# Row-order key loads, an activation in three instructions and paired PSUM banks in a fused window-attention and feed-forward kernel

## The chip, the cores and the metric

The kernel runs on one core of one Trainium2 chip. The metric is device time in microseconds (us) from the first to the last instruction of the launch, as the median of several runs. The core's engines are named as in the profile: PE (TensorE, matrix products), PEld (its weight loads), DVE (VectorE), ACT (ScalarE), POOL (GpSimd, which here also issues the input DMAs) and SP (SyncE, which issues the output DMAs). Each engine works through its own instructions in program order and waits on semaphores for the others.

## What is computed

Eight batches of eight heads, 576 positions, 64 dimensions: attention in a symmetric window of 32 positions, then a feed-forward layer with a smooth ReLU ("SMELU") on the 4608 tokens of 512 features. Cut to what matters:

```python
def _attn_ref(q, k, v):                      # (8, 8, 576, 64) each
    scores = (1.0 / np.sqrt(D)) * np.matmul(q, k.transpose(0, 1, 3, 2))
    mask = np.abs(pos[:, None] - pos[None, :]) <= 32
    scores = np.where(mask, scores, -1000000000.0)
    attn = np.exp(scores - np.max(scores, axis=-1, keepdims=True))
    attn = attn / (np.sum(attn, axis=-1, keepdims=True) + 1e-09)
    return np.matmul(attn, v)

def _moe_ref(x, w_in, w_out):                # (4608, 512), (512, 2048), (2048, 512)
    h = x @ w_in
    g = np.where(h >= 1, h, np.where(h <= -1, 0.0, (h + 1) ** 2 / 4.0))
    return g @ w_out                         # x: heads side by side, (4608, 512)
```

## The kernel before

All matrix work is in bf16 with fp32 sums. The program is one list of slots, `a` from -1 on, and each engine executes its instructions in the order in which the slots write them (a manual schedule; no planner reorders). A slot of the steady part holds, in this order on PE: four matmuls of the first layer into one PSUM bank `hp` (L257), one group of score matmuls into `sc` (L180), four matmuls of the second layer into `op` (L277), and either a group of transposes into `tp` (L152) or the denominators and numerators of half a head pair, `dn` and `nm` (L197, L198, L206). Attention runs ahead of the feed-forward layer by 29 slots: slots -1 to 28 hold attention alone, the first layer starts in slot 29, the second layer 16 slots later, attention ends in slot 139, the first layer in slot 172, and 16 slots of the second layer alone close the program. The pattern repeats every eight slots, which handle one `m`, that is four heads in two pairs `i`; a slot with `a` odd has a `dn`/`nm` half, an even one a transpose group, and every slot but multiples of four has scores.

What feeds PE, by engine:

- POOL issues the loads of `qn`, `kn` (L89, two each for one `m`) and `vz` (L96, two for one `i`), converting to bf16, at the start of fixed slots: `q` and `k` of one `m` every eight slots, `v` of one `i` every four. Between them it multiplies the exponentials by the window's mask (L189). DMAs issued by POOL go round eight landing semaphores, so each issue waits until the eighth last has landed.
- `q` and `k` are loaded with nine consecutive positions for each partition (p j order), which makes long runs in DRAM. DVE then copies them to `qj` and `kj` so that two heads stand side by side (the relay, L140); PE transposes 9 blocks of 128x128 in two groups (5 and 4 blocks) for each of `q` and `k`; DVE evacuates the transposed `q` to `qT` (L157, one copy of 640 or 512 elements a group) and ACT the transposed `k` to the zero-padded `kz` (L164, four copies of 64 partitions a group), both scattering elements with a stride so that positions come out in order.
- ACT takes the exponentials `pt` (L188) and the reciprocals of the denominators as exp(-ln) (`lr`, `rc`, L212 and L213); DVE multiplies `nm` by `rc` into `xT` (L217), the feed-forward layer's input, one slot after `nm` was written.
- SMELU is written as max(h,-1) + (0.5 min(max(h,-1),1) - 0.5)^2: DVE clamps `hp` to `c` (L260), ACT squares it to `s` (L268), and DVE adds max(hp,-1) in the next slot to give `gT` (L271).
- ACT evacuates `op` to `osb` every fourth slot (L281) and SP sends it out (L283).

The eight PSUM banks are three for `hp` and one each for `op`, `sc`, `tp`, `nm` and `dn`. A bank is written again only when its reader has finished.

## Time and profile before

| What | us |
|---|---|
| Median of 3 runs | 472.46 (472.14 to 472.97) |
| The profiled execution | 473.16 |
| Its span, first to last instruction | 471.4 |
| PE busy | 347.5 (74%) |
| DVE busy | 311.1 (66%) |
| ACT busy | 268.9 (57%) |
| POOL busy, computing and issuing | 175.0 (37%) |

A share of the whole span is an average over stages: the loading and the first attention slots, two rounds of eight slots with the first layer but without the second, ten rounds with everything, the rounds in which attention fades out, the two layers alone, and the second layer alone. So the profile is read stage by stage. A round takes eight slots, and where nothing but PE limits it the starts of consecutive groups of matmuls follow each other without a gap; a gap has a releaser, which the trace names.

### The profile page before, as it was taken

How to read it: one execution, taken by the hardware profiler on the slowest of the kernel's cores; microseconds unless marked ns; L12 is line 12 of the kernel's file. 1: busy time of each engine (PE TensorE's matmuls, PEld its weight loads, DVE VectorE, ACT ScalarE, POOL GpSimd, SP SyncE). 2: the span in 40 equal slices, each digit the busy share in tenths (PEclk: the TensorE clock that was granted, in tenths of full speed). 3: DMA queues.
4: the chain of work that ended last, by engine and by line, in shares of the span. 5: the costliest groups of instructions: out<-in, count | busy, mean ns of one | idle time of the engine just before them, and what ended most of it. 6: DMA issues, size and time to landing. Idle time of an engine off the chain costs nothing.

```text
span 471.4 us, 6061 instructions
## 1 busy us (share of the span) xinstructions
PE 347.5 (74%) x2176; PEld 183.1 (39%) x2176; DVE 311.1 (66%) x441; ACT 268.9 (57%) x533; POOL 175.0 (37%) x236
## 2 busy tenths in 40 slices
PE   0135458567979787878787879787878999798976
PEld 0024334333535343434343435343444543343432
DVE  5633556868777777777777777777776666666610
ACT  1057557575767666666666666666667743333320
POOL 8647586262717171717171726232223200000000
PEclk9999999895999999999999989999999999999999
DMA  9999873343445353535363626220000010101011
GB/s 97 170 160 177 116 76 37 39 42 35 52 69 63 60 69 52 69 53 78 43 76 45 88 33 89 32 37 22 24 22 24 22 46 22 45 24 42 26 44 67
DMA packets 54909, 28.17 MB, mean 60 GB/s; under 512 B 39520, under 2 KB 49760, under 8 KB 54880
## 3 DMA queue, kind: packets, MB, share of 16 engines
q0 software_dynamic: 49696, 18.36, 35.1%
q1 hardware_dynamic: 5184, 9.44, 5.4%
q8 instruction: 17, 0.28, 0.2%
q14 instruction: 12, 0.10, 0.1%
HBM read 36.70 MB, written 9.44 MB: 98 GB/s over the span
## 4 chain that ended last, share of the span: by engine, by line
PE 39%; ACT 23%; DVE 19%; issue 15%; POOL 2%; ACTq 0%; DVEq 0%; POOLq 0%
PE op L277 18%; PE hp L257 13%; ACT kz L164 11%; DVE c L260 10%; ACT s L268 6%; ACT osb L281 4%; DVE qT L157 4%; DVE gT L271 3%; PE tp L152 3%; ACT pt L188 2%; PE nm L206 2%; PE sc L180 1%; POOL vz L96 1%; DVE xT L217 1%; PE dn L197 1%
## 5 line engine op out<-in xcount | busy, mean ns | idle before, releaser
L277 PE MATMUL op<-w_out,gT 128*128 128x512 bf16 x576 | 148.3, 384 | 36.2 <-ACT osb L281 36.2
L271 DVE SCALAR_TENSOR_TENSOR gT<-hp,s 128x512 bf16<-128x512 f32 x144 | 104.3, 724 | 104.4 <-ACT s L268 104.4
L268 ACT ACTIVATE s<-c 128x512 f32<-128x512 f32 x144 | 90.5, 628 | 137.7 <-DVE c L260 137.2
L257 PE MATMUL hp<-xT,w_in 128*128 128x512 bf16 x576 | 153.8, 390 | 2.0 <-DVE xT L217 1.8
L189 POOL TENSOR_TENSOR pt<-pt,maskp 128x352 bf16<-128x352 bf16 (+1 forms) x96 | 84.3, 881 | 185.5 <-ACT pt L188 185.0
L260 DVE TENSOR_SCALAR c<-hp 128x512 f32<-128x512 f32 x144 | 97.8, 679 | 3.5 <-PE hp L257 3.5
L164 ACT COPY kz<-tp 64x320 bf16<-64x320 bf16 (+1 forms) x128 | 77.4, 711 | 31.2 <-PE tp L152 30.9
L157 DVE COPY qT<-tp 128x640 bf16<-128x640 bf16 (+1 forms) x32 | 86.3, 2696 | 9.7 <-PE tp L152 9.7
L277 PEld LDWEIGHTS <-gT 128*128 128x128 bf16 x576 | 54.6, 98 | 93.8 <-issue 44.2
L257 PEld LDWEIGHTS <-w_in 128*128 128x128 bf16 x576 | 53.3, 100 | 45.8 <-issue 4.6
L96 POOL DMA_DIRECT2D vz<-in_v_dram x64 | 50.0, 789 | 11.2 <-DMA w_in<-in_moe_w_in_dram 10.4
L188 ACT ACTIVATE pt<-sc 128x352 bf16<-128x352 f32 (+1 forms) x96 | 44.7, 465 | 12.0 <-PE sc L180 11.1
L180 PE MATMUL sc<-qT,kz 128*128 128x128 bf16 (+1 forms) x288 | 34.1, 233 | 17.7 <-ACT pt L188 17.7
L180 PEld LDWEIGHTS <-kz 128*128 128x128 bf16 x288 | 25.7, 107 | 44.8 <-issue 29.5
L152 PE MATMUL tp<-ident,qj 128*128 128x128 bf16 x144 | 15.1, 240 | 33.9 <-DVE qj L140 16.4
L217 DVE TENSOR_TENSOR xT<-nm,rc 128x288 bf16<-128x288 f32 x64 | 29.1, 454 | 15.0 <-ACT rc L213 9.0
L152 PE MATMUL tp<-ident,kj 128*128 128x128 bf16 x144 | 15.4, 243 | 26.4 <-DVE kj L140 23.8
L206 PE MATMUL nm<-pt,vz 128*128 128x128 bf16 (+2 forms) x320 | 29.1, 228 | 2.1 <-DVE xT L217 2.1
L213 ACT ACTIVATE rc<-lr 128x288 f32<-128x288 f32 x64 | 28.3, 443 | 2.0
L281 ACT COPY osb<-op 128x512 f32<-128x512 f32 x36 | 20.5, 569 | 14.9 <-PE op L277 14.9
L152 PEld LDWEIGHTS <-qj 128*128 128x128 bf16 x144 | 11.9, 107 | 40.8 <-DVE qj L140 18.4
L206 PEld LDWEIGHTS <-vz 128*128 128x128 bf16 x320 | 23.3, 107 | 9.5 <-issue 5.9
(29 smaller groups left out, 160.2 us busy)
## 6 DMA issues: line engine op xcount, KB each, us to landing
out_dram<-osb SPq DMA_DIRECT2D x36, 256.0 KB, 2.0
qn<-in_q_dram POOLq DMA_DIRECT2D x32, 144.0 KB, 3.3
kn<-in_k_dram POOLq DMA_DIRECT2D x32, 144.0 KB, 5.2
vz<-in_v_dram POOLq DMA_DIRECT2D x64, 72.0 KB, 3.4
w_in<-in_moe_w_in_dram POOLq DMA_DIRECT2D x1, 2048.0 KB, 15.6
w_out<-in_moe_w_out_dram POOLq DMA_DIRECT2D x1, 2048.0 KB, 15.3
```

What stands on the lines that cost most here:

```text
L96: nc.gpsimd.dma_start(out=vz[i % 8][h:128:2, :, 64 * h:64 * h + 64], in_=v[b, 2 * hp + h].rearrange("(c p) d -> p c d", p=64))
L152: nc.tensor.transpose(ps[:, j - j0], src[:, j].rearrange("p h d -> p (h d)"), ident)
L157: nc.vector.tensor_copy(qT[m].rearrange("d g (p j) -> d j g p", j=NC)[:, j0:j1], ps[:, :n].rearrange("d j (g p) -> d j g p", g=2))
L164: nc.scalar.copy(kz[2 * (m % 2) + g][r].rearrange("d (p j t) -> d t p j", j=NC, t=2)[:, h, :, j0:j1], ps[r, :n].rearrange("d j (g p) -> d ...
L180: nc.tensor.matmul(ps[:, off:off + q1 - q0], kz[2 * (m % 2) + gg][:, 128 * c:128 * c + 128], qT[m][:, gg, q0:q1], start=True, stop=True)
L189: nc.gpsimd.tensor_mul(pt[i][:, seg], pt[i][:, seg], maskp[:, seg])
L206: nc.tensor.matmul(nm[:, q0 - lo:q1 - lo], vz[i % 8][:, c], pt[i][:, pcol(c, q0):pcol(c, q1)], start=n == 0, stop=n == len(parts) - 1, ski ...
L257: nc.tensor.matmul(hp, w_in[:, kk, 128 * f:128 * f + 128], xT[:, kk, TB * blk:TB * blk + TB], start=kk == 0, stop=kk == 3)
L260: nc.vector.tensor_scalar(c1, hp, -1.0, 1.0, op0=ALU.max, op1=ALU.min)
L268: nc.scalar.activation(s1, c1, AF.Square, scale=0.5, bias=-0.5)
L271: nc.vector.scalar_tensor_tensor(gT[blk][:, f], hp, -1.0, s1, op0=ALU.max, op1=ALU.add)
L277: nc.tensor.matmul(op, gT[blk - 1][:, ff, 128 * tt:128 * tt + 128], w_out[:, ff], start=ff == 0, stop=ff == 15)
```

## The change

- `k` is loaded in row order (64 consecutive positions over the partitions, nine chunks), one DMA for each head, so four issues instead of two for one `m`; `kn` then has the layout that the transposes read, and the relay of `k` falls away. `v` and `k` stand in two halves of 64 partitions, one for each head, instead of interleaved, and the masks and the matrix of ones are built for that.
- The relay of `q` moves from DVE to POOL.
- `qT` is evacuated by ACT (two copies a group), `kz` by DVE (four copies a group, contiguous runs of 64).
- SMELU becomes max(h,r) min(r,1) with r = relu(0.5 h + 0.5) from ACT (`rr`), then two DVE instructions in the same slot: `yy` = max(hp, rr) and `gT` = min(rr,1) yy.
- PSUM: `hp` has two banks instead of three, `op` two instead of one, and `sc` and `tp` share two (one tag) instead of having one each.

```diff
-    ps_h = ctx.enter_context(tc.tile_pool(name="ps_h", bufs=3, space=bass.MemoryType.PSUM))
-    ps_o = ctx.enter_context(tc.tile_pool(name="ps_o", bufs=1, space=bass.MemoryType.PSUM))
-    ps_s = ctx.enter_context(tc.tile_pool(name="ps_s", bufs=1, space=bass.MemoryType.PSUM))
-    ps_t = ctx.enter_context(tc.tile_pool(name="ps_t", bufs=1, space=bass.MemoryType.PSUM))
+    ps_h = ctx.enter_context(tc.tile_pool(name="ps_h", bufs=2, space=bass.MemoryType.PSUM))
+    ps_o = ctx.enter_context(tc.tile_pool(name="ps_o", bufs=2, space=bass.MemoryType.PSUM))
+    ps_s = ctx.enter_context(tc.tile_pool(name="ps_s", bufs=2, space=bass.MemoryType.PSUM))
...
+        for g in range(2):
+            for h in range(2):
+                nc.gpsimd.dma_start(out=kn[m][64 * g:64 * g + 64, :, h],
+                                    in_=k[b, 4 * qd + 2 * g + h].rearrange("(c p) d -> p c d", p=64))
...
-                out=vz[i % 8][h:128:2, :, 64 * h:64 * h + 64],
+                out=vz[i % 8][64 * h:64 * h + 64, :, 64 * h:64 * h + 64],
...
-    def relay(m, t):
-
-        src, dst = ((qn, qj), (kn, kj))[t // 2]
-        dst[m] = qkj.tile([128, NC, 2, D], BF, name="qj" if t < 2 else "kj")
-        nc.vector.tensor_copy(dst[m].rearrange("p j h d -> p h j d"),
-                              src[m].rearrange("p h (j d) -> p h j d", d=D))
+    def relay(m):
+
+        qj[m] = qjp.tile([128, NC, 2, D], BF, name="qj")
+        nc.gpsimd.tensor_copy(qj[m].rearrange("p j h d -> p h j d"),
+                              qn[m].rearrange("p h (j d) -> p h j d", d=D))
...
-        ps = ps_t.tile([128, 5, 128], BF, name="tp")
+        ps = ps_s.tile([128, 5, 128], BF, name="tp", tag="sc")
...
-                nc.vector.tensor_copy(
-                    qT[m].rearrange("d g (p j) -> d j g p", j=NC)[:, j0:j1],
-                    ps[:, :n].rearrange("d j (g p) -> d j g p", g=2))
...
+        if t < 2:
+            for g in range(2):
+                nc.scalar.copy(
+                    qT[m][:, g].rearrange("d (p j) -> d p j", j=NC)[:, :, j0:j1],
+                    ps[:, :n].rearrange("d j (g p) -> d g p j", g=2)[:, g])
+        else:
+            for h in range(2):
+                for g in range(2):
                     r = slice(64 * h, 64 * h + 64)
...
+                    nc.vector.tensor_copy(kz[2 * (m % 2) + g][r, j0:j1, h],
+                                          ps[r, :n].rearrange("d c (g p) -> d g c p", g=2)[:, g])
...
-            if t % 2 == 0:
-                att_r[8 * m + 2 * t - 1] = (m, t)
+        att_r[8 * m - 1] = m
...
-            c1 = ewp.tile([128, TB], FP, name="c1")
-            nc.vector.tensor_scalar(c1, hp, -1.0, 1.0, op0=ALU.max, op1=ALU.min)
+
+            rr = ewp.tile([128, TB], FP, name="rr")
+            yy = ewp.tile([128, TB], FP, name="yy")
+            nc.scalar.activation(rr, hp, AF.Relu, scale=0.5, bias=0.5)
+            nc.vector.tensor_max(yy, hp, rr)
+            nc.vector.scalar_tensor_tensor(gT[blk][:, f], rr, 1.0, yy, op0=ALU.min, op1=ALU.mult)
```

On POOL, at the end of the start-up loads, before:

```order
L96 DMA vz_118<-in_v_dram 64x9x64 x2
L131 DMA w_out<-in_moe_w_out_dram 128x16x512
L89 DMA qn<-in_q_dram 64x2x576 x2
L89 DMA kn<-in_k_dram 64x2x576 x2
L189 TENSOR_TENSOR pt<-pt,maskp 128x352 x2
```

And now, at the same place:

```order
L97 DMA vz_115<-in_v_dram 64x9x64 x2
L129 DMA w_out<-in_moe_w_out_dram 128x16x512
L137 COPY qj<-qn 128x2x9x64 x2
L87 DMA qn<-in_q_dram 64x2x576 x2
L91 DMA kn<-in_k_dram 64x9x64 x4
L182 TENSOR_TENSOR pt<-pt,maskp 128x352 x2
```

The relays of the first two `m`, on which PE's first transposes wait, now stand on POOL behind all start-up loads; before they stood on DVE.

On POOL, one later round of eight slots, before:

```order
L189 TENSOR_TENSOR pt<-pt,maskp 128x384
L89 DMA qn<-in_q_dram 64x2x576 x2
L89 DMA kn<-in_k_dram 64x2x576 x2
L189 TENSOR_TENSOR pt<-pt,maskp 128x352
L96 DMA vz_113<-in_v_dram 64x9x64 x2
L189 TENSOR_TENSOR pt<-pt,maskp 128x352
```

And now:

```order
L182 TENSOR_TENSOR pt<-pt,maskp 128x384
L137 COPY qj<-qn 128x2x9x64
L87 DMA qn<-in_q_dram 64x2x576 x2
L91 DMA kn<-in_k_dram 64x9x64 x4
L182 TENSOR_TENSOR pt<-pt,maskp 128x352
L97 DMA vz_110<-in_v_dram 64x9x64 x2
```

A relay and two more DMA issues stand between the mask product that ends one round and the one that opens the next.

On DVE, a stretch of the same stage around a `q` evacuation, before (`c` and `s` carry running numbers):

```order
L260 TENSOR_SCALAR c_1643<-hp 128x512
L217 TENSOR_TENSOR xT<-nm,rc 128x288
L157 COPY qT<-tp 128x5x128
L271 SCALAR_TENSOR_TENSOR gT<-hp,s_1646 128x512
L260 TENSOR_SCALAR c_1669<-hp 128x512
```

And now around a `k` evacuation:

```order
L248 TENSOR_TENSOR yy<-hp,rr 128x512
L249 SCALAR_TENSOR_TENSOR gT<-rr,yy 128x512
L208 TENSOR_TENSOR xT<-nm,rc 128x288
L160 COPY kz_106<-tp 64x5x64
L160 COPY kz_107<-tp 64x5x64
L160 COPY kz_106<-tp 64x5x64
L160 COPY kz_107<-tp 64x5x64
L248 TENSOR_TENSOR yy<-hp,rr 128x512
```

The product `gT` follows its own slot's `yy` at once, and `xT` comes behind both; the one long copy is replaced by four short ones.

## Rows read from the trace of the kernel before

**Rows 1.** Six stages: us, busy of PE, PEld, DVE, ACT, POOL; PEclk, DMA share, GB/s.

```profile
0.00:69.50 69.50, 22.64 (x170) 17.02 (x171) 37.03 (x49) 28.33 (x56) 48.40 (x73) 1.00 1.06 135
69.50:114.10 44.60, 29.88 (x195) 15.91 (x193) 32.79 (x45) 28.73 (x58) 21.32 (x28) 0.90 0.40 40
114.10:346.60 232.50, 189.94 (x1282) 101.28 (x1281) 173.80 (x241) 157.42 (x320) 97.44 (x126) 0.98 0.38 53
346.60:384.20 37.60, 33.83 (x218) 17.75 (x216) 25.18 (x42) 27.05 (x55) 7.85 (x9) 1.00 0.08 29
384.20:451.00 66.80, 56.71 (x257) 24.98 (x256) 42.12 (x67) 25.04 (x42) 0.00 (x0) 1.00 0.09 32
451.00:471.50 20.50, 14.45 (x64) 6.14 (x63) 0.22 (x1) 2.34 (x4) 0.00 (x0) 0.97 0.17 64
```

**Rows 2.** Timeline of PE in one round: start us, us, engine, line, operation.

```profile
214.20 0.33 PE L180 MATMUL sc<-qT,kz 128*128 128x128 bf16 x3
214.36 1.03 PE L277 MATMUL op<-w_out,gT 128*128 128x512 bf16 x4
215.23 0.29 PE L197 MATMUL dn<-pt,ones 128*128 128x288 bf16 x1
...
215.70 1.03 PE L257 MATMUL hp<-xT,w_in 128*128 128x512 bf16 x4
...
217.43 0.44 PE L152 MATMUL tp<-ident,qj 128*128 128x128 bf16 x5
217.70 1.03 PE L257 MATMUL hp<-xT,w_in 128*128 128x512 bf16 x4
```

**Rows 3.** Waits of the whole span: who for whom, us in total, times, longest.

```profile
PE op L277 <- ACT osb L281: 36.2, 34, 2.0
```

**Rows 4.** Groups of instructions: count, busy us, mean ns, idle before and its releaser.

```profile
L271 DVE SCALAR_TENSOR_TENSOR gT<-hp,s 128x512 bf16<-128x512 f32 x144 | 104.3, 724 | 104.4 <-ACT s L268 104.4
L268 ACT ACTIVATE s<-c 128x512 f32<-128x512 f32 x144 | 90.5, 628 | 137.7 <-DVE c L260 137.2
...
L260 DVE TENSOR_SCALAR c<-hp 128x512 f32<-128x512 f32 x144 | 97.8, 679 | 3.5 <-PE hp L257 3.5
L164 ACT COPY kz<-tp 64x320 bf16<-64x320 bf16 (+1 forms) x128 | 77.4, 711 | 31.2 <-PE tp L152 30.9
L157 DVE COPY qT<-tp 128x640 bf16<-128x640 bf16 (+1 forms) x32 | 86.3, 2696 | 9.7 <-PE tp L152 9.7
...
L188 ACT ACTIVATE pt<-sc 128x352 bf16<-128x352 f32 (+1 forms) x96 | 44.7, 465 | 12.0 <-PE sc L180 11.1
...
L217 DVE TENSOR_TENSOR xT<-nm,rc 128x288 bf16<-128x288 f32 x64 | 29.1, 454 | 15.0 <-ACT rc L213 9.0
...
L189 POOL TENSOR_TENSOR pt<-pt,maskp 128x352 bf16<-128x352 bf16 x64 | 55.1, 862 | 149.6 <-ACT pt L188 149.2
...
L189 POOL TENSOR_TENSOR pt<-pt,maskp 128x384 bf16<-128x384 bf16 x32 | 29.4, 919 | 35.8 <-ACT pt L188 35.8
...
L89 POOL DMA_DIRECT2D kn<-in_k_dram x32 | 19.5, 626 | 1.7 <-DMA w_out<-in_moe_w_out_dram 1.6
```

**Rows 5.** Start-up on PE and POOL: start us, us, operation, idle before and its releaser.

```profile
16.37 0.71 PE L152 MATMUL tp<-ident,qj 128*128 128x128 bf16 x5 [16.37 <-DVE qj L140]
```

**Rows 6.** Start-up on POOL alone, the large loads: start us, us, operation.

```profile
13.97 0.78 POOL L127 DMA_DIRECT2D w_in<-in_moe_w_in_dram  x1
...
29.83 3.78 POOL L96 DMA_DIRECT2D vz<-in_v_dram  x5 [10.39 <-DMA w_in<-in_moe_w_in_dram]
33.57 1.20 POOL L131 DMA_DIRECT2D w_out<-in_moe_w_out_dram  x1
```

**Rows 7.** The relay of `k` on DVE: duration min/median/max, first and last start.

```profile
L140 DVE COPY kj<-kn x16: 436/448/1660, 22.8 to 345.8; 128x1152 bf16<-128x1152 bf16 x16
```

**Rows 8.** Timeline around the longest of them: start us, us, engine, operation.

```profile
51.73 1.66 DVE L140 COPY kj<-kn 128x1152 bf16<-128x1152 bf16 x1
52.20 1.96 POOL L189 TENSOR_TENSOR pt<-pt,maskp 128x352 bf16<-128x352 bf16 x2
```

More of the change, by code (lines that the diff above doesn't have):

```diff
@@ L52 @@
     qkn = ctx.enter_context(tc.tile_pool(name="qkn", bufs=3))
-    qkj = ctx.enter_context(tc.tile_pool(name="qkj", bufs=2))
+    qjp = ctx.enter_context(tc.tile_pool(name="qjp", bufs=2))
     qtp = ctx.enter_context(tc.tile_pool(name="qtp", bufs=2))
@@ L73 @@
     xT = const.tile([128, 4, NT], BF, name="xT")
-    kz = [const.tile([128, 2 * S], BF, name=f"kz{i}") for i in range(4)]
+    kz = [const.tile([128, NC, 2, 64], BF, name=f"kz{i}") for i in range(4)]
     vz = [const.tile([128, NC, 128], BF, name=f"vz{i}") for i in range(8)]
@@ L83, in load_qk @@
         b, qd = divmod(m, 2)
-        for src, dst, nm in ((q, qn, "qn"), (k, kn, "kn")):
-            t = qkn.tile([128, 2, S], BF, name=nm)
-            dst[m] = t
-            for g in range(2):
-                h0 = 4 * qd + 2 * g
-                nc.gpsimd.dma_start(
-                    out=t[64 * g:64 * g + 64],
-                    in_=src[b, h0:h0 + 2].rearrange("h (p j) d -> p h (j d)", j=NC))
+        qn[m] = qkn.tile([128, 2, S], BF, name="qn")
+        kn[m] = qkn.tile([128, NC, 2, D], BF, name="kn")
+        for g in range(2):
+            h0 = 4 * qd + 2 * g
+            nc.gpsimd.dma_start(out=qn[m][64 * g:64 * g + 64],
+                                in_=q[b, h0:h0 + 2].rearrange("h (p j) d -> p h (j d)", j=NC))
+        for g in range(2):
+            for h in range(2):
+                nc.gpsimd.dma_start(out=kn[m][64 * g:64 * g + 64, :, h],
+                                    in_=k[b, 4 * qd + 2 * g + h].rearrange("(c p) d -> p c d", p=64))
     def load_v(i):
@@ L118 @@
         nc.vector.tensor_copy(maskp[:, pcol(c, q0):pcol(c, q0) + q1 - q0], mask1[:, j0:j0 + q1 - q0])
-    nc.gpsimd.memset(ones2, 1.0)
-    ev = smp.tile([128, 64, 2], FP, name="ev")
-    par = smp.tile([128, 2], FP, name="par")
-    nc.vector.tensor_copy(ev, ident.rearrange("p (a b) -> p a b", b=2))
-    nc.vector.reduce_sum(par, ev.rearrange("p a b -> p b a"), axis=mybir.AxisListType.X)
-    for h in range(2):
-        nc.vector.tensor_scalar_mul(ones2[:, 64 * h:64 * h + 64], ones2[:, 64 * h:64 * h + 64], par[:, h:h + 1])
     nc.gpsimd.dma_start(out=w_in, in_=moe_w_in.rearrange("(ko ki) f -> ki ko f", ki=128))
@@ L174, in scores @@
             pt[i] = ptp.tile([128, PW], BF, name="pt")
-        ps = ps_s.tile([128, 512], FP, name="sc")
+        ps = ps_s.tile([128, 512], FP, name="sc", tag="sc")
         off = 0
@@ L185, in scores @@
         seg = slice(first, first + off)
-        def finish():
-            nc.scalar.activation(pt[i][:, seg], ps[:, :off], AF.Exp, scale=D ** -0.5)
-            nc.gpsimd.tensor_mul(pt[i][:, seg], pt[i][:, seg], maskp[:, seg])
-        return finish
+        nc.scalar.activation(pt[i][:, seg], ps[:, :off], AF.Exp, scale=D ** -0.5)
+        nc.gpsimd.tensor_mul(pt[i][:, seg], pt[i][:, seg], maskp[:, seg])
     def pv(i, hf):
@@ L207, in pv, with mul @@
                              start=n == 0, stop=n == len(parts) - 1, skip_group_check=True)
-        def act():
-            lr = smp.tile([128, HALF], FP, name="lr")
-            rc = smp.tile([128, HALF], FP, name="rc")
-            nc.scalar.activation(lr, dn, AF.Ln)
-            nc.scalar.activation(rc, lr, AF.Exp, scale=-1.0)
-            def mul():
-                b, hp = divmod(i, H // 2)
-                nc.vector.tensor_mul(xT[:, hp, b * S + lo:b * S + hi], nm, rc)
-            return mul
-        return act
+        lr = smp.tile([128, HALF], FP, name="lr")
+        rc = smp.tile([128, HALF], FP, name="rc")
+        nc.scalar.activation(lr, dn, AF.Ln)
+        nc.scalar.activation(rc, lr, AF.Exp, scale=-1.0)
+        def mul():
+            b, hp = divmod(i, H // 2)
+            nc.vector.tensor_mul(xT[:, hp, b * S + lo:b * S + hi], nm, rc)
+        return mul
     A0 = 9
@@ L264 @@
         if a in att_s:
-            scores(*att_s[a])()
-        if hp is not None:
-            s1 = ewp.tile([128, TB], FP, name="s1")
-            nc.scalar.activation(s1, c1, AF.Square, scale=0.5, bias=-0.5)
-            def stt(hp=hp, s1=s1, blk=blk, f=f):
-                nc.vector.scalar_tensor_tensor(gT[blk][:, f], hp, -1.0, s1, op0=ALU.max, op1=ALU.add)
+            scores(*att_s[a])
         if 1 <= blk <= NBLK and mm >= 0:
@@ L284 @@
         if a in att_r:
-            relay(*att_r[a])
+            relay(att_r[a])
         if a in att_x:
```

42 lines of the change are left out of this document (17 added, 25 removed).

## The prediction

> **What bounds the kernel now.** I read the six stages first, then the chain of waits, then PE's timeline inside one round, then the costliest groups. Ten rounds of eight slots take 232.5 us, 23.25 each, in which PE is busy 19.0, DVE 17.4, ACT 15.7 and POOL 9.7 [rows 1]: no engine fills the round, so something between them does. PE's own need comes from its timeline where nothing holds it [rows 2]: `op` to `dn` is 0.87 us and an `hp` group costs the same, `sc` 0.16, a `dn`/`nm` half 0.47, a transpose group of five blocks 0.27, one of four in proportion 0.22. A round is 16 x 0.865 + 6 x 0.16 + 4 x 0.47 + 1.0 = 17.7 us. The other 5.6 us are waits of PE: for the single `op` bank until ACT has emptied it (36.2 us in all, 34 times) [rows 3], and for transposes behind one `tp` bank, which is emptied by `qT` copies of 2.7 us on DVE or by four `kz` copies of 0.71 us on ACT [rows 4], with the activation's own steps queued behind these. In the stage with the two layers alone the same bank shows undiluted: 66.8 us for 32 slots [rows 1], 2.09 each against 2 x 0.865 = 1.73.
>
> **The change, part by part, in one steady round.** *PE* does the same matmuls, 17.7 us. *DVE* loses two `qT` copies (5.4 us) and two relays (0.45 each at the median [rows 7]). It gains eight `kz` copies, which no row shows. A 288-element read of PSUM takes 0.454 us and a 512-element one 0.679 [rows 4], 1.0 ns an element, so 320 and 256 elements are 0.49 and 0.42: eight come to 3.6; half of that, 1.8, is the lower bound if packed bf16 goes at two elements a step, as the relay does at better than two; I take 3.2. `yy` is priced as `c` (0.679) and `gT` stays at 0.72, but `gT` now waits for the `yy` just ahead of it, so the two no longer overlap with their neighbours: about 1.36 a slot, 10.9 a round. With four `xT` (1.8) that is 15.9 us. *ACT* loses eight `kz` copies (5.7 us) and gains four `qT` copies; they read the same pattern at 128 instead of 64 partitions, so 0.71 each is the row for them (0.46, what an exponential of 352 or 384 elements takes, is the other end [rows 4]): 15.7 - 5.7 + 2.8 = 12.8. The relu is priced as the square, 0.63 [rows 4], and no longer waits for DVE.
>
> *POOL* gains the relay of `q` and two DMA issues. Four `kn` issues in the form of `vz`, 3.78 / 5 = 0.76 us [rows 6], replace two of 0.626 [rows 4]: +1.8. The relay on POOL is the unknown. The mask product's two sizes, 352 and 384 elements, take 0.862 and 0.919 [rows 4]: 1.78 ns an element and 0.24 fixed. At that rate 1152 elements cost 2.3 us; with one operand to read instead of two, half the slope, 1.3. I take 1.7. POOL is then 9.7 + 1.8 + 1.7 = 13.2 busy.
>
> So PE's 17.7 is the floor and DVE comes next. Two things keep a round above it. First, the relay stands in POOL's queue behind the mask product of slot 7 and ahead of the six DMA issues of the next round. Slot 7 begins; `hp` is there after 1.1 us, the relu takes 0.6, the exponential 0.5, the mask product 0.9: 3.1, with the relay 4.8. PE reaches the transposes after slot 7 (0.865 + 0.16 + 0.865 + 0.47) and two groups of the next, at 4.1, so it waits about 0.8 with handovers (nothing at a relay of 1.0 us, 1.4 at 2.3). Behind it on POOL the six issues (4.3 us) end before PE needs the next mask products. `kn` can be loaded only when PE has transposed the old one; that is two slots back and costs nothing, except in the start-up. Second, `xT` now comes behind `yy` and `gT`, so the single `nm` bank is free about 0.7 us after the next half could write it, and the second of two `hp` banks is free just as PE wants it. I put 0.7 on these. A round is then 17.7 + 0.8 + 0.7 = **19.2 us**, and the stage 192 instead of 232.5. The wait for `op` goes entirely; late next are the relay and DVE.
>
> **The start-up pays.** PE's first transpose started at 16.4 us, released by the relay on DVE [rows 5]. On POOL the first relays stand behind every start-up load. `w_in` was issued at 13.97 [rows 6]; ahead of it now are two `m` of `kn` at +1.8 each and more mask instructions (about 1.1), so 18.7. POOL then stood idle 10.39 us until `w_in` landed, at about 29.8 [rows 6], since issues go round eight landing semaphores. It meets that wait again, now until about 34, then issues seven `vz` (5.3) and `w_out` (1.2 [rows 6]) and starts the first relay near 40.6. From there POOL paces attention: two relays to 44.0; the next `kn` issues wait until the first `m` is transposed, near 46, and end at 49.1; six mask products with the latencies between them, to 56.5; the third relay, 58.2; six issues, 62.5; six products (5.3) and four `vz` issues (3.0), 70.8; the fourth relay, 72.5. PE then needs five more slots, transposes and scores in turn through two banks, with the last `dn`, `rc` and `xT`, about 6.5 us in all: slot 29 at **79** instead of 69.5 us, +9.5 (+4 with a relay of 1.3 and `w_in` landing earlier, +15 with 2.3 and later). The faster evacuations, which would shorten this stage, are hidden behind POOL.
>
> **The sum.** Start-up 79. Two rounds without the second layer: PE needs little, and DVE's 15.9 is the largest load, so 16 each, 32 (44.6 before). Ten rounds, 192 (232.5). The fading rounds: 16 x 1.73 + 9 x 0.16 + 8 x 0.47 + 0.2 = 33.1, say 33.5 (37.6). The two layers alone: 32 x 1.73 = 55.4 (66.8). The second layer alone: 16 x 0.865 = 13.8, and behind it the last evacuation and store, which stay: 20.5 less PE's 14.45 [rows 1] and less three handovers of the bank at about 0.7 (an evacuation of 512 elements, priced as the square's 0.63) is 3.9; 17.7 (20.5). Total 409.6. The profiled execution took 473.16 for its span of 471.4, so 1.8 lie around it: 411.4. It was 0.7 above the median of the runs, so the forecast is **410.7 us**. PE's clock is granted at 0.98 and more in all but the second stage, at 0.90 there [rows 1], that is at its upper level of 2.4 GHz but for short stretches; I keep it.
>
> **Rivals.** *VectorE and GpSimd block each other (B).* The longest relay of `k` took 1.66 us instead of 0.45 [rows 7], and a mask product of 0.86 began 0.47 after its start; it ended 0.33 after that product did [rows 8]. So this DVE instruction, which moves 1152 elements in 0.45 us when alone, was held until the POOL instruction had ended. Before, `gT` read one operand from PSUM; now it reads `rr` and `yy`, both in SBUF. In the walk the exponential ends 0.2 us before `yy` does, so the mask product starts just ahead of `gT`, and if it shuts it out, `gT` loses 0.65 us in six slots of eight and about 0.5 at the relay: 15.9 + 4.4 = 20.3 on DVE, above PE, and with two `hp` banks PE follows it. With a gap of 1.0, 21.3 a round: 10 x 2.1 + 3 more, **435 us** (422 to 452). Against it: only this fast copy shows it, and `gT` goes at one element a step. A third of the loss would leave DVE at 17.4, under PE's 17.7; that much the forecast bears. The Trainium skill, SBUF — State Buffer, section Who interferes with whom, states that a Vector instruction with two SBUF inputs contends with a GpSimd instruction that reads SBUF, the later one blocking fully; by that rule B is the case, in the part where the queues really meet; rows 8 agree for the wide copy, and no run here shows it yet for two inputs.
>
> *Everything closes up (C).* The relay takes 1.3 us, `kz` goes packed, nothing blocks: 17.9 a round, start-up 76: 411 - 13 - 3 - 1 = **394 us** (385 to 400).
>
> *The relay on GpSimd is far slower than its product (D): slower than before.* It lies in series with the first transposes of every round: four times before slot 29 and in 12 rounds after it, 16 in all. The forecast is 61.8 us below the time before, so 61.8 / 16 = 3.9 us on top of 1.7 uses it up: from 5.6 us, 4.9 ns an element, the change loses; at 6.0 it gives 411 + 16 x 4.3 = **480 us**. For it: no row shows a copy of 18 separate runs on POOL. Against: the only slope on POOL is 1.78 ns with two operands.
>
> *The doubled banks don't free PE (E).* `sc` and `tp` share two banks, so a score group may wait for four `kz` copies on DVE, and `hp` has one bank less. Of the 36.2 us for `op` [rows 3] the two last stages hold 11.4 + 2.8; if the other 22 come back under another name, it is **433 us**. For it: in the walk two handovers have no slack. Against: the two layers alone have neither `sc` nor `tp`, and there an `hp` bank is free 2.5 us after its matmuls began, of 3.46.
>
> **How the numbers follow.** A 0.57, B 0.22, C 0.12, D 0.05, E 0.04. A alone runs from 399 (rounds of 18.2) to 424 (rounds of 20.3). The range goes from 392, which takes in half of C, to 442, two thirds of B and most of E: 0.56 + 0.06 + 0.15 + 0.03. Within 0.2%, about what a measurement of this kernel can tell from no change, lies next to nothing: 0.02; faster 0.93; slower 0.05.
>
> **What would show it.** Right: the first transpose near 42 us, slot 29 near 79; no wait of `op` for `osb`; rounds of 19 us with PE over 90% busy; the last 48 slots at 1.73 and 0.865. The relay's row on POOL prices D and C at once. B would show as `gT` means well above 0.72 or long idle time of DVE ahead of `gT` released by nothing that it needs, and PE waiting for `yy` at `hp`. The forecast is wrong above all if the relay is off by a microsecond (16 us), or if POOL's start-up is not in the order that I followed.

## The result and the profile after

The changed kernel takes **393.44 us** (median of 4 runs, 392.84 to 393.75) where the kernel before takes 472.3: a ratio of 0.8327, 95% interval 0.8313 to 0.8342. The profiled execution took 393.38 us for a span of 391.7. The forecast was 410.7 and its range 392 to 442: the sign is right, the time lies at the range's lower edge, 17 us faster than the forecast, outside the 399 to 424 of case A and at the 394 of case C.

First the stages. The columns are those of [rows 1]; the boundaries are the first matmuls of slots 29, 45, 125, 141 and 173, as there, but for slot 45. Its first matmul starts at 104.59 us and its fourth waits 1.58 us for `xT`; its boundary stands 1 us ahead of its relu instead, as those of slots 29, 125 and 141 do. Counted from its first matmul, the two rounds take 33.5 us and the ten 181.0.

```profile
0.00:71.00 71.00, 21.16 (x169) 16.88 (x171) 17.01 (x52) 19.60 (x48) 59.48 (x90) 0.93 1.21 129
71.00:106.40 35.40, 23.86 (x191) 13.64 (x194) 31.38 (x56) 22.72 (x53) 31.24 (x39) 1.00 0.76 58
106.40:285.60 179.20, 175.87 (x1253) 98.52 (x1278) 166.09 (x280) 129.00 (x280) 121.28 (x152) 1.00 0.61 69
285.60:318.60 33.00, 32.79 (x214) 17.61 (x216) 28.65 (x49) 21.86 (x45) 7.85 (x9) 1.00 0.09 33
318.60:373.90 55.30, 55.04 (x253) 25.10 (x257) 44.58 (x66) 23.74 (x40) 0.00 (x0) 1.00 0.10 39
373.90:391.70 17.80, 13.65 (x63) 6.11 (x63) 1.34 (x2) 2.93 (x5) 0.00 (x0) 1.00 0.20 74
```

| Stage | before | forecast | after |
|---|---|---|---|
| start-up, to slot 29 | 69.5 | 79 | 71.0 |
| two rounds without the second layer | 44.6 | 32 | 35.4 |
| ten steady rounds | 232.5 | 192 | 179.2 |
| fading rounds | 37.6 | 33.5 | 33.0 |
| two layers alone | 66.8 | 55.4 | 55.3 |
| second layer alone | 20.5 | 17.7 | 17.8 |

In the ten rounds PE is busy 175.87 of 179.20 us, and 25 matmul records are missing (1253 against 1278 weight loads), so it is as good as full: 0.98 where [rows 1] had 0.82. The distances between the relus give 17.75 us for eight of the ten rounds and 18.62 for the other two.

The groups that answer to [rows 4] and [rows 7] (count, busy us, mean ns, idle before; the last line gives the relay's minimum, median and maximum):

```profile
L249 DVE SCALAR_TENSOR_TENSOR gT<-rr,yy 128x512 bf16<-128x512 f32 x144 | 130.3, 905 | 5.1
L248 DVE TENSOR_TENSOR yy<-hp,rr 128x512 f32<-128x512 f32 x144 | 99.2, 689 | 26.7 <-ACT rr L247 24.4
L160 DVE COPY kz<-tp 64x320 bf16<-64x320 bf16 (+1 forms) x128 | 33.2, 298 | 25.8 <-PE tp L149 25.3
L153 ACT COPY qT<-tp 128x320 bf16<-128x320 bf16 (+1 forms) x64 | 24.8, 454 | 47.9 <-PE tp L149 47.7
L91 POOL DMA_DIRECT2D kn<-in_k_dram x64 | 47.9, 791 | 0.9 <-PE tp L149 0.9
```

```profile
L137 POOL COPY qj<-qn x16: 1137/1144/1153, 38.2 to 275.2; 128x1152 bf16<-128x1152 bf16 x16
```

Three prices stand out: a `kz` copy at 0.30 us, a `qT` copy at 0.45 and a relay at 1.14 are all cheaper than forecast; of the dearer ones `gT` is the one that matters, 0.905 for 0.724.

The waits inside the ten rounds (who for whom, us in total, times, longest) hold nothing of [rows 3]: `op` no longer waits for `osb`. The last line is the only one of PE's matmuls.

```profile
...
ACT rr L247 <- PE hp L242: 28.4, 56, 2.3
...
ACT osb L264 <- PE op L260: 5.3, 20, 0.3
PEld L149 <- POOL qj L137: 4.0, 10, 0.4
...
PE hp L242 <- DVE xT L208: 3.0, 3, 1.6
```

It is the other engines that wait for PE now. PE's side waits in the last two lines: 0.4 us for the relay, once a round, by the weight load; and for `xT` at the start of three blocks of tokens.

The start-up on POOL and the first transposes on PE (start us, us, operation, idle before and its releaser) answer to [rows 5, 6]:

```profile
18.23 0.78 POOL L125 DMA_DIRECT2D w_in<-in_moe_w_in_dram  x1
...
31.36 0.73 POOL L97 DMA_DIRECT2D vz<-in_v_dram  x1 [7.42 <-DMA w_in<-in_moe_w_in_dram]
...
36.92 1.21 POOL L129 DMA_DIRECT2D w_out<-in_moe_w_out_dram  x1
38.18 2.23 POOL L137 COPY qj<-qn 128x1152 bf16<-128x1152 bf16 x2
...
45.43 3.37 POOL L182 TENSOR_TENSOR pt<-pt,maskp 128x352 bf16<-128x352 bf16 x4
...
51.67 1.14 POOL L137 COPY qj<-qn 128x1152 bf16<-128x1152 bf16 x1
...
64.93 1.15 POOL L137 COPY qj<-qn 128x1152 bf16<-128x1152 bf16 x1
```

```profile
39.37 1.14 PE L149 MATMUL tp<-ident,qj 128*128 128x128 bf16 x9 [39.37 <-POOL qj L137]
```

As forecast, the first relays stand behind every start-up load and PE begins 23 us later than before; the stage is 1.5 us longer all the same, not 9.5.

### The profile page after: what moved, and what is told of

It reads as the page before. It is cut to its first block, busy times and chain, and to the rows that moved or that the text cites. A ratio compares the mean times of both kernels' runs of the same rounds, so it can differ in the third digit from the quotient of the medians.

```text
span 391.7 us, 6070 instructions
## 1 busy us (share of the span) xinstructions
PE 322.4 (82%) x2136; PEld 177.9 (45%) x2176; DVE 289.0 (74%) x501; ACT 219.8 (56%) x469; POOL 219.9 (56%) x288
## 4 chain that ended last, share of the span: by engine, by line
PE 71%; POOL 11%; DVE 9%; DMA 3%; issue 2%; ACT 2%; another core or an unknown queue 1%; ACTq 0%; POOLq 0%
PE op L260 30%; PE hp L242 28%; DMA w_in<-in_moe_w_in_dram 3%; POOL vz L97 3%; PE nm L198 3%; DVE gT L249 3%; PE tp L149 3%; POOL pt L182 3%; PE sc L174 3%; DVE yy L248 3%; POOL kn L91 3%; PE dn L189 2%; PE dn L190 2%; DVE vz L106 1%; DVE xT L208 1%
## 5 line engine op out<-in xcount | busy, mean ns | idle before, releaser
L242 PE MATMUL hp<-xT,w_in 128*128 128x512 bf16 x555 | 146.0, 379 | 4.2 <-DVE xT L208 3.0
L260 PE MATMUL op<-w_out,gT 128*128 128x512 bf16 x557 | 142.3, 379 | 0.7
L249 DVE SCALAR_TENSOR_TENSOR gT<-rr,yy 128x512 bf16<-128x512 f32 x144 | 130.3, 905 | 5.1
L247 ACT ACTIVATE rr<-hp 128x512 f32<-128x512 f32 x144 | 86.1, 598 | 76.7 <-PE hp L242 71.6
L248 DVE TENSOR_TENSOR yy<-hp,rr 128x512 f32<-128x512 f32 x144 | 99.2, 689 | 26.7 <-ACT rr L247 24.4
L160 DVE COPY kz<-tp 64x320 bf16<-64x320 bf16 (+1 forms) x128 | 33.2, 298 | 25.8 <-PE tp L149 25.3
L149 PE MATMUL tp<-ident,qj 128*128 128x128 bf16 x144 | 15.2, 242 | 44.6 <-POOL qj L137 43.8
L153 ACT COPY qT<-tp 128x320 bf16<-128x320 bf16 (+1 forms) x64 | 24.8, 454 | 47.9 <-PE tp L149 47.7
L91 POOL DMA_DIRECT2D kn<-in_k_dram x64 | 47.9, 791 | 0.9 <-PE tp L149 0.9
L203 ACT ACTIVATE lr<-dn 128x288 f32<-128x288 f32 x64 | 26.5, 414 | 19.8 <-PE dn L190 19.8
L198 PE MATMUL nm<-pt,vz 128*128 128x128 bf16 (+2 forms) x320 | 27.7, 221 | 7.5 <-DVE xT L208 7.5
L264 ACT COPY osb<-op 128x512 f32<-128x512 f32 x36 | 21.1, 587 | 19.4 <-PE op L260 16.6
L198 PEld LDWEIGHTS <-vz 128*128 128x128 bf16 x320 | 22.2, 103 | 17.8 <-issue 12.5
```

Of the source, the lines that this page charges most:

```text
L91: nc.gpsimd.dma_start(out=kn[m][64 * g:64 * g + 64, :, h], in_=k[b, 4 * qd + 2 * g + h].rearrange("(c p) d -> p c d", p=64))
L149: nc.tensor.transpose(ps[:, j - j0], src[:, j].rearrange("p h d -> p (h d)"), ident)
L198: nc.tensor.matmul(nm[:, q0 - lo:q1 - lo], vz[i % 8][:, c], pt[i][:, pcol(c, q0):pcol(c, q1)], start=n == 0, stop=n == len(parts) - 1, ski ...
L242: nc.tensor.matmul(hp, w_in[:, kk, 128 * f:128 * f + 128], xT[:, kk, TB * blk:TB * blk + TB], start=kk == 0, stop=kk == 3)
L247: nc.scalar.activation(rr, hp, AF.Relu, scale=0.5, bias=0.5)
L248: nc.vector.tensor_max(yy, hp, rr)
```

## Experiments

Ratios are to the kernel before on the same chip; a difference in us is the difference of two ratios times 472.3. The kernel after stands at 0.8327.

### Which part is worth what: the evacuations

The contiguous copy of `k` went from ACT to DVE, the scattered copy of `q` from DVE to ACT in two pieces. The first experiment puts only this back; `k` is still loaded in row order, so its copy stays contiguous.

```diff
-            for g in range(2):
-                nc.scalar.copy(
-                    qT[m][:, g].rearrange("d (p j) -> d p j", j=NC)[:, :, j0:j1],
...
+            nc.vector.tensor_copy(
+                qT[m].rearrange("d g (p j) -> d j g p", j=NC)[:, j0:j1],
...
-                    nc.vector.tensor_copy(kz[2 * (m % 2) + g][r, j0:j1, h],
+                    nc.scalar.copy(kz[2 * (m % 2) + g][r, j0:j1, h],
```

> The changed kernel with only the evacuating engines exchanged: qT again by DVE in one scattered copy a group (2.4 and 3.0 us), kz by ACT in contiguous runs. If PE's floor of 17.7 us a round holds only because the evacuations went where they are cheap, DVE gets 5.4 - 2.4 = 3.0 us a round more than its 16.5 and becomes the bound: rounds of 19.5 to 21, 415 to 435 us. If the row order of k and the relay on POOL alone made the difference, the rounds stay under 18 us and the time under 400 us.

449.42 us, ratio 0.9528 (0.9481 to 0.9575): 56.7 us slower than after, more than the 415 to 435 expected. Its groups and, last, its ten steady rounds (columns as above):

```profile
L152 DVE COPY qT<-tp 128x640 bf16<-128x640 bf16 (+1 forms) x32 | 86.3, 2707 | 26.5 <-PE tp L149 26.5
L248 DVE SCALAR_TENSOR_TENSOR gT<-rr,yy 128x512 bf16<-128x512 f32 x144 | 137.8, 957 | 5.8 <-DVE yy L247 0.5
```

```profile
L159 ACT COPY kz<-tp 64x320 bf16<-64x320 bf16 (+1 forms) x128 | 44.1, 393 | 47.1 <-PE tp L149 46.2
```

```profile
119.60:340.10 220.50, 188.79 (x1277) 101.13 (x1277) 202.83 (x219) 139.42 (x316) 126.73 (x152) 0.97 0.50 56
```

On DVE the scattered copy of `q` costs 86.3 us in 32 pieces; on ACT the same elements cost 24.8 (the groups of after). A round takes 22.05 us, in which VectorE is busy 20.3 and PE 18.9: with `qT` (5.4 us a round) and the new `gT` in one queue, VectorE is the fullest engine, 0.92 busy, and PE waits behind it. The runs stand in a row: 472.3 us before; 456.6 with the new activation alone (below); 449.4 here, which adds `k`'s row order, the relays' move and the banks; 393.4 with the swap. In this order the swap is 57 of the kernel's 79 us, by far the largest part, and all that is neither swap nor activation is 7. That it is worth so much because the new `gT` (0.957 here) loads VectorE more than the old one is argued, not shown: on the kernel before, where VectorE had 17.4 of 23.25 us, the swap was not run alone.

### The second `op` bank

On the kernel after, `op` gets one bank and `hp` three, as before. On the kernel before, the reverse:

```diff
-    ps_h = ctx.enter_context(tc.tile_pool(name="ps_h", bufs=2, space=bass.MemoryType.PSUM))
-    ps_o = ctx.enter_context(tc.tile_pool(name="ps_o", bufs=2, space=bass.MemoryType.PSUM))
+    ps_h = ctx.enter_context(tc.tile_pool(name="ps_h", bufs=3, space=bass.MemoryType.PSUM))
+    ps_o = ctx.enter_context(tc.tile_pool(name="ps_o", bufs=1, space=bass.MemoryType.PSUM))
```

> The changed kernel with one bank for op and three for hp, as before the change; nothing else differs. If the second op bank is what freed PE (the prediction's step), the wait of op for its evacuation returns: about 11 us in the two-layer stage, 3 in the last one and up to 22 in the rounds, 405 to 430 us. If the prompt evacuation freed it, because ACT no longer holds a square behind the clamp on DVE, op finds its bank empty after the next hp group (0.865 us against 0.59 for the copy and handovers), and only the last stage pays, 395 to 398 us.

> The kernel before with two op banks and two hp banks, nothing else. If the single op bank is what PE waited for, its 36 us come back: 440 to 455 us. If the activation's order on the engines is the cause, the wait moves from op to hp, as in the changed kernel with the old activation (rounds of 16.36 us in the two-layer stage, as before): 465 to 476 us.

With one bank the kernel after takes 396.8 us, 0.8384 (0.8351 to 0.8417): 2.7 us more. Its steady rounds stay at 17.75 and the two layers alone at 13.81 for eight slots. Of the 36.2 us of [rows 3] this is all that comes back, in the whole span, beside three banks for `hp`:

```profile
PE op L260 <- ACT osb L264: 2.8, 4, 0.7
```

The kernel before with two banks takes 465.77 us, 0.9855 (0.9827 to 0.9883), 6.8 less. The wait for `op` is gone and another stands in its place, PE's wait for a free `hp` bank:

```profile
PE hp L257 <- DVE gT L271: 55.2, 71, 2.7
```

So a second bank for `op`, taken from `hp` since no other is free, only moves the wait. What ends it is the new activation: with that alone on the kernel before, one bank for `op` and three for `hp`, PE's wait falls to this:

```profile
PE op L271 <- ACT osb L275: 2.8, 4, 0.7
```

ACT came to `op` late because the square ahead of it in its queue waited for VectorE's clamp (137.2 us in all, [rows 4]); the relu reads `hp` itself.

### The activation

On the kernel after, the clamp, square and sum of before are put back (two `hp` banks stay); on the kernel before, the new form alone:

```diff
-            rr = ewp.tile([128, TB], FP, name="rr")
-            yy = ewp.tile([128, TB], FP, name="yy")
-            nc.scalar.activation(rr, hp, AF.Relu, scale=0.5, bias=0.5)
-            nc.vector.tensor_max(yy, hp, rr)
-            nc.vector.scalar_tensor_tensor(gT[blk][:, f], rr, 1.0, yy, op0=ALU.min, op1=ALU.mult)
+            c1 = ewp.tile([128, TB], FP, name="c1")
+            nc.vector.tensor_scalar(c1, hp, -1.0, 1.0, op0=ALU.max, op1=ALU.min)
...
+            nc.scalar.activation(s1, c1, AF.Square, scale=0.5, bias=-0.5)
...
+                nc.vector.scalar_tensor_tensor(gT[blk][:, f], hp, -1.0, s1, op0=ALU.max, op1=ALU.add)
```

> The changed kernel with the activation written as before (clamp on DVE, square on ACT, sum on DVE one slot later). If PE is the bound and the freed evacuations are what made the difference, DVE stays under the round and the time is 393 to 400 us. If the activation's order on the engines made it, two hp banks are released a slot later, rounds go to 19 us and more, and the time to 410 to 430 us. In both cases the sum reads one operand from PSUM, so its mean should fall back from 905 to about 700 ns if the mask products hold the form with two SBUF operands.

> The kernel before with the new activation alone: relu on ACT, maximum and product on DVE in the same slot, one op bank. The two-layer stage should fall to 13.8 us for eight slots, 11 us in all, and the last one stay. In the rounds DVE still does the scattered qT copies and both relays: with its 17.4 us plus 2 to 4 held by the mask products it stays the bound, 20 to 23 us a round. 425 to 460 us. If the evacuations were not needed, the rounds fall under 19 us and the time under 415.

Put back, it costs 5.5 us: 399.76, 0.8444 (0.8407 to 0.8481). The steady rounds are no slower (17.65); the two layers alone go from 13.8 to between 16.2 and 16.4 us for eight slots. Of the two lines from this kernel the first is a wait, the second a group:

```profile
PE hp L246 <- DVE gT L261: 12.3, 42, 1.1
```

```profile
L261 DVE SCALAR_TENSOR_TENSOR gT<-hp,s 128x512 bf16<-128x512 f32 x144 | 99.6, 692 | 74.7 <-ACT s L258 73.9
```

The old chain DVE, ACT, DVE holds an `hp` bank across three handovers, and with two banks PE waits for it. On the kernel before the new form gains 15.4 us (456.59, 0.9673, 0.9629 to 0.9717), most of it in the same last stages (13.8 for eight slots). Its steady rounds stay at 22.65 to 24.6 in the profiled execution, which at 460.28 was the slowest of the four. PE's longest waits in them are for the two relays, which there stand on VectorE in one queue with the `qT` copies:

```profile
PE tp L152 <- DVE kj L140: 18.2, 10, 1.8
...
PE tp L152 <- DVE qj L140: 11.6, 10, 1.2
```

| Part | alone on the kernel before | taken out of the kernel after |
|---|---|---|
| second `op` bank, taken from `hp` | -6.8 | +2.7 |
| activation | -15.4 | +5.5 |
| evacuations swapped (with `k` in row order on both sides) | not run | +56.7 |

`k`'s row order, the end of its relay and the two banks that `sc` and `tp` share were not run by themselves.

### The relay

The walk in the prediction says that the relay on POOL lies in series with PE's transposes. The copy is simply done twice.

```diff
+        nc.gpsimd.tensor_copy(qj[m].rearrange("p j h d -> p h j d"),
+                              qn[m].rearrange("p h (j d) -> p h j d", d=D))
```

> The changed kernel with the relay of q done twice on POOL, +1.14 us for each of 16. If the relay lies in series with PE's transposes, as the prediction's walk has it (in the trace after, the transposes wait 0.4 us for it in every round), each round pays nearly all of it: 16 x 1.1, about 411 us. If POOL's idle time hides it, only the start-up pays, four relays: about 398 us.

415.81 us, 0.8795 (0.8755 to 0.8836): 22.1 us for 16 copies, 1.4 each, and steady rounds of 19.3. PE's waits in the whole span name it (40.7 us is the first one, in the start-up):

```profile
PE tp L151 <- POOL qj L139: 65.1, 15, 40.7
```

So the place was right; at 1.14 us the relay just has no cost left to show in the ten rounds. That it belongs on POOL was asked by moving it back to DVE:

```diff
-        nc.gpsimd.tensor_copy(qj[m].rearrange("p j h d -> p h j d"),
+        nc.vector.tensor_copy(qj[m].rearrange("p j h d -> p h j d"),
```

> Kernel after, but the relay of q (the copy that puts q's heads in the transposes' order) is done by VectorE, throughout, as the relay of the kernel before was. Theory: the relay lies in series with PE's transposes, 0.4 us a round of PE's wait at GpSimd's 1.14 us each. On VectorE it should take 0.44 (the row of the kernel before) and free GpSimd; VectorE has 1.2 us a round to spare. So the ten rounds stay at 17.7, the start-up loses up to 3 us because the relays no longer stand behind the loads on GpSimd, and the time is 388 to 393. Rival: VectorE's queue holds the relay behind gT and the kz copies, or GpSimd's products hold the copy as they held the relay of the kernel before at 1.66: rounds 18.0 to 18.5 and 395 to 402.

399.66 us, 0.8445 (0.8416 to 0.8474), 5.6 slower: the rival. The copy itself takes 0.49 us at the median, but it queues behind `gT` (in one round it starts at 154.47 us, behind a `gT` that began at 153.86). Waits between 143 and 285 us, eight rounds, first of this kernel, then of the kernel after:

```profile
PEld L149 <- DVE qj L137: 6.8, 8, 1.1
PE tp L149 <- DVE qj L137: 2.9, 8, 0.6
```

```profile
PEld L149 <- POOL qj L137: 3.2, 8, 0.4
```

On DVE the wait is 0.85 a round, and 0.36 of it is idle time of PE's matmuls, which matches rounds of 18.16 instead of 17.75. In the kernel after the same wait of 0.4 belongs to the weight load alone; PE's matmuls don't stop.

### VectorE and GpSimd

Case B said that the mask product on POOL holds `gT`. Here the products are left out (the window's mask is then not applied), nothing else.

```diff
-        nc.gpsimd.tensor_mul(pt[i][:, seg], pt[i][:, seg], maskp[:, seg])
```

> The changed kernel without the mask products on POOL (the window's mask is left out, so every position of the loaded blocks counts). If PE's matmuls are the floor, the rounds stay at 17.7 us and only the start-up gets shorter, by up to 13 us (15 products): 380 to 388 us. If the blocking between DVE and POOL still costs time, the rounds get shorter too. If the products are what holds gT, its mean falls from 905 ns to about 720, what is left coming from the relay and the DMA issues.

388.76 us, 0.8212 (0.818 to 0.8243), 5.4 less, just above the range expected. `gT` falls from 0.905 to 0.745:

```profile
L248 DVE SCALAR_TENSOR_TENSOR gT<-rr,yy 128x512 bf16<-128x512 f32 x144 | 107.3, 745 | 5.0
```

The gain lies ahead of the ten rounds: slot 29 comes 6.1 us earlier, and the next two rounds take 2.1 less. The ten rounds take 3.4 more. Their fastest are 17.65, and others are up to 19.3, where PE waits for `xT` at the start of a block, behind a `gT` that the relay holds (1.22 us):

```profile
PE hp L241 <- DVE xT L207: 4.6, 3, 2.1
```

The mechanism shows in the timeline of the kernel after, DVE first, then POOL (start us, us, engine, line, operation):

```profile
163.72 0.69 DVE L249 SCALAR_TENSOR_TENSOR gT<-rr,yy 128x512 bf16<-128x512 f32 x1
165.22 1.08 DVE L249 SCALAR_TENSOR_TENSOR gT<-rr,yy 128x512 bf16<-128x512 f32 x1
168.33 1.24 DVE L249 SCALAR_TENSOR_TENSOR gT<-rr,yy 128x512 bf16<-128x512 f32 x1
170.20 0.69 DVE L249 SCALAR_TENSOR_TENSOR gT<-rr,yy 128x512 bf16<-128x512 f32 x1
171.89 0.97 DVE L249 SCALAR_TENSOR_TENSOR gT<-rr,yy 128x512 bf16<-128x512 f32 x1
176.24 1.55 DVE L249 SCALAR_TENSOR_TENSOR gT<-rr,yy 128x512 bf16<-128x512 f32 x1
```

```profile
164.90 0.85 POOL L182 TENSOR_TENSOR pt<-pt,maskp 128x352 bf16<-128x352 bf16 x1
167.88 1.14 POOL L137 COPY qj<-qn 128x1152 bf16<-128x1152 bf16 x1
170.21 2.99 POOL L91 DMA_DIRECT2D kn<-in_k_dram  x4
175.48 1.76 POOL L182 TENSOR_TENSOR pt<-pt,maskp 128x352 bf16<-128x352 bf16 x2
```

Where a product started 0.3 us ahead, `gT` took 1.08 and ended 0.55 after it; behind the relay, 1.24 and again 0.55 after; behind two products in a row, 1.55. With neither it takes 0.69, as it does with one SBUF operand in the kernel with the old activation (0.692 over the whole run). In the ten rounds `gT` takes 79.71 us in 80 pieces, 7.97 a round against 8 x 0.692 = 5.54 alone: 2.4 us a round lost. DVE is then busy 16.6 us of a round of 17.92 and PE doesn't feel it. The blocking is real, and in these ten rounds hidden.

### The start-up

Is it PE's late first transpose or POOL's queue that sets slot 29 at 71 us? First only the relays of the first two pieces are put ahead of `w_in`:

```diff
+    relay(0)
+    relay(1)
     nc.gpsimd.dma_start(out=w_in, in_=moe_w_in.rearrange("(ko ki) f -> ki ko f", ki=128))
...
-        att_r[8 * m - 1] = m
+        if m > 1:
+            att_r[8 * m - 1] = m
```

> The changed kernel with the relays of the first two m ahead of the load of w_in on POOL. PE's first transpose then starts near 21 us instead of 39. If POOL's own queue paces the start-up, as the prediction has it, slot 29 comes earlier only by the two relays and a short wait, 2 to 4 us: 389 to 392 us. If PE's late start paces it, slot 29 comes up to 15 us earlier: 376 to 382 us.

394.93 us, 0.8354 (0.8332 to 0.8377): no gain, and neither of the two times expected. PE transposes 20 us earlier, and slot 29 comes at 72.7 by the same count, because the products of the mask still stand on POOL behind the weights:

```profile
PE dn L190 <- POOL pt L183: 20.5, 2, 17.7
```

Then POOL's queue is thinned as well: the weights in quarters, between the products, `q` and `k` one round later and `v` half a round.

```diff
-    nc.gpsimd.dma_start(out=w_in, in_=moe_w_in.rearrange("(ko ki) f -> ki ko f", ki=128))
-    load_qk(2)
-    for i in range(4, 8):
-        load_v(i)
-    nc.gpsimd.dma_start(out=w_out, in_=moe_w_out.rearrange("(ko ki) f -> ki ko f", ki=128))
...
+    relay(0)
+    relay(1)
+    load_qk(2)
...
-        loads.setdefault(8 * m - 16, []).append((load_qk, m))
+        loads.setdefault(8 * m - 8, []).append((load_qk, m))
...
-        loads.setdefault(4 * i - 14, []).append((load_v, i))
+        loads.setdefault(4 * i - 10, []).append((load_v, i))
+    for at, fn, n in ((8, load_w_in, 0), (12, load_v, 4), (14, load_v, 5), (18, load_w_in, 1), (18, load_v, 6),
+                      (20, load_v, 7), (25, load_w_in, 2), (29, load_w_in, 3), (33, load_w_out, 0),
+                      (35, load_w_out, 1), (37, load_w_out, 2), (41, load_w_out, 3)):
+        loads.setdefault(at, []).append((fn, n))
```

> Kernel after, but GpSimd's start-up queue is thinned: the relays of the first two pieces stand ahead of the feed-forward weights, w_in and w_out are loaded in four quarters each, spread over slots 8 to 41, and the loads of q, k and v stand some rounds later. Nothing else is changed. Theory: the 71 us before slot 29 are paced by GpSimd's queue, in which the issues of the large weights wait and the mask's products stand behind them (moving the relays alone gave slot 29 at 72.7). Then slot 29 comes near 52 to 56 and the whole takes 375 to 380 us, the ten rounds still at 17.75. Rival: the bytes themselves pace the start-up (the weights must be there before the first feed-forward block, wherever they are issued): then slot 29 stays within 3 us of 71, or the waits turn up in the first rounds as blocks waiting for w_in, and the time stays at 390 or above.

**380.6 us**, 0.8052 (0.803 to 0.8074): 13.0 faster than after, the best of all. Its stages (columns as above), with the same events as boundaries:

```profile
0.00:55.10 55.10, 21.29 (x171) 17.05 (x172) 18.60 (x52) 19.55 (x48) 53.55 (x82) 0.81 1.10 96
55.10:94.40 39.30, 23.85 (x194) 13.70 (x193) 33.89 (x56) 22.61 (x53) 35.69 (x45) 1.00 1.21 131
94.40:273.60 179.20, 177.19 (x1278) 98.52 (x1278) 166.54 (x280) 129.03 (x280) 126.93 (x160) 1.00 0.67 74
```

Slot 29 comes 15.9 us earlier, the next two rounds are 3.9 longer since loads have moved into them, and the ten rounds take 179.20 to the hundredth, with PE, all records present, busy 177.19. POOL is busy 53.55 of the first 55.1 us. In the kernel after it is busy 59.48 of 71.0: so of the 15.9 us some 10 are idle time of POOL (7.42 of it the wait for `w_in` shown above) and 6 are work moved behind slot 29. How much the bytes that moved with the issues count by themselves was not run.

Last, the relay three slots earlier in this kernel, so that nothing in a round waits for it:

```diff
-            att_r[8 * m - 1] = m
+            att_r[8 * m - 4] = m
```

> Kernel e8_start_loads_spread with one table entry changed: GpSimd's relay of a piece of q stands three slots earlier (8m-4, before 8m-1), so that PE's transposes find it done. Theory: in the ten rounds PE has no real idle time at the relay (the 0.4 us of the relay's wait is the weight load's, which lies beside the matmul before it), so they stay at 17.75, which is PE's own work; in the start-up the two waits of PE for the relay (3.8 and 3.5 us in the trace of e8_start_loads_spread) shrink, and slot 29 comes 0 to 5 us earlier than its 56.1: 375 to 381 us. Rival: the 0.4 us is PE's idle time, then the ten rounds fall to 17.35 and the time to 371 to 377. Second rival: GpSimd's order is what counts, and the earlier relay holds up the products of the mask: 382 to 386.

385.97 us, 0.8165 (0.8147 to 0.8183), 5.3 slower than without: the second rival's time. The transposes' wait is gone. That rival's mechanism, PE waiting for mask products, shows only ahead of the ten rounds; the line is of this kernel's whole span:

```profile
PE dn L196 <- POOL pt L188: 12.4, 6, 3.5
```

In the ten rounds, most of them 18.05, PE's matmuls wait for `xT` alone. Products and relay now meet more of `gT`, which takes 88.1 us there instead of 80.1; two held ones in a row stand ahead of one `xT` in each round (the first line is PE's wait for it, then DVE in one round):

```profile
PE nm L204 <- DVE xT L214: 2.2, 9, 0.2
...
144.09 1.82 DVE L260 SCALAR_TENSOR_TENSOR gT<-rr,yy 128x512 bf16<-128x512 f32 x1
...
146.54 1.65 DVE L260 SCALAR_TENSOR_TENSOR gT<-rr,yy 128x512 bf16<-128x512 f32 x1
```

So what was hidden in the kernel after comes to PE here.

## Why the prediction was right, and what in it was not

**The frame held.** PE's floor of 17.7 us a round, worked out from [rows 2], is what is measured: 17.65 to 17.75 in several kernels. The waits between engines were the 5.6 us that could be had. The last three stages, priced from PE's rows alone but for the final stores, came within 0.5 us: 33.0, 55.3 and 17.8. That the total lies in the range, by 1.4 us, is partly luck: the start-up and the ten rounds came 20.8 us below the forecast, and the range reached down to 392 only to take in half of case C.

**The ten rounds, 192 against 179.2, are the largest miss.** Two terms failed. The relay's wait, 0.8, rested on a relay of 1.7, between 1.3 and 2.3. It takes 1.14, below the lower end. The walk itself set the wait at nothing at 1.0 us, and close to that it landed: 0.4 us at the weight load, none at the matmuls. The other, 0.7 for `nm` and for the `hp` banks, was a margin without a row: `nm` doesn't wait in these rounds, and what is there is `hp`'s wait for `xT` at the start of three blocks, (18.62 - 17.75) x 2 = 1.7 us in two rounds and 1.58 in slot 45 at the stage's edge. The two terms were 1.5 x 10 = 15 us of the forecast; 2.2 of them came, or 4.0 counted from slot 45's first matmul.

**The start-up, 79 against 71.0.** POOL came out of its wait for `w_in` at 31.36, forecast near 34, and the first relay started at 38.18, forecast 40.6. The first two relays took 2.2 where 3.4 was forecast, and the third and fourth at 1.14 for 1.7 are another 1.1. That is 4.7 of the 8 us. Another 1.2 is the six mask products with the latencies between them, 6.2 (45.43 to 51.67) for 7.4, and 1.6 is what PE needs behind the fourth relay, 4.9 (66.08 to 71.0) for 6.5; the last 0.5 is spread over the steps between. That POOL paces this stage is borne out by the two start-up kernels: PE 20 us earlier gained nothing, a thinner queue 15.9 us.

**The two rounds without the second layer, 35.4 against 32** (33.5 by slot 45's first matmul). That DVE is the largest load was right: it is busy 31.38 us, 15.7 a round for 15.9, and the chain of work that ended last runs along it for 71% of the stage and along POOL for some 11%, at the start. Shares of the stage, by line:

```profile
by line: DVE gT L249 31.6%; DVE yy L248 24.3%; DVE kz L160 7.9%; DVE xT L208 7.3%; PE hp L242 7.3%; ACT rr L247 6.9%; POOL pt L182 6.6%; POOL vz L97 4.0%; issue 3.1%; PE nm L198 2.9%; PE dn L190 0.8%
```

The step that failed is that a round takes DVE's load and no more: DVE stands idle for 4.0 of the 35.4 us, mostly until a relu is there. Nor is the blocking hidden here: `gT` takes 0.897 on the mean of its 16, 3.3 us above 0.692 each; the cheap `kz` happened to make up for most of it. With the products gone the two rounds take 2.1 less.

**The wait for `op` "goes entirely": right, for a wrong reason.** I credited the second bank with 11.4 + 2.8 and up to 22 more. The two bank kernels price it at 2.7 and 6.8 us, and the new activation alone, with one bank, leaves 2.8 of the 36.2 us. What the second bank is worth in the kernel after is what the prediction priced for the last stage alone, three handovers at 0.7.

**DVE's and ACT's own prices.** `kz` goes at 0.315 us for 320 and 0.281 for 256 elements, near the packed lower bound (eight: 2.4; I took 3.2 between 1.8 and 3.6). `qT` on ACT is the 0.46 that was the other end, not 0.71. In the ten rounds both were hidden behind PE, so neither moved their sum. What the prediction did not see is how the parts hang together: it took the 5.4 us of `qT` off VectorE as one entry among others, and that entry is what keeps VectorE below PE. With `qT` put back, VectorE is at 20.3 of 22.05 us a round.

**The rivals.** Case B's mechanism is real: 2.4 us a round, where I priced 4.4. It needed DVE above 17.7; DVE came to 16.6, since its load without the loss was 14.2 (16.6 less 2.4) instead of 15.9; the cheap `kz` is 0.8 of that. The prediction set the turning point at a third of the loss; at a little over half it still did not decide. With `qT` on VectorE the held `gT` (0.957) stands in the fullest queue, and with the relay three slots earlier 0.8 us a round more of it slowed PE by 0.3. The Trainium skill, SBUF — State Buffer, section Who interferes with whom, states that a Vector instruction with two SBUF inputs contends with a GpSimd instruction that reads SBUF, and calls the shared ports an exclusive lock; the traces agree (0.69 us alone, 1.08 to 1.55 beside products), but the rule gives the loss of an instruction, not whether the engine has room for it. By that rule alone the time would have been case B's 435. [rows 8] fit it less well than the prediction says: the relay's record starts 0.47 us ahead of the product that it waited for, and POOL was issuing a load of `v` until 52.18. Case C names the time and half the reasons: a relay under 1.3 and packed `kz`, yes; "nothing blocks", no. Case D's slow relay did not come (1.14 against its 5.6); its place in series did, as the doubled relay showed. Case E fell: the wait came back in no other name.
